# Fused attention and feed-forward kernel: order and gates of the loads, place of one small operation, size of the dummy matmuls

## The chip, the core and the metric

The kernel runs on one core of a Trainium2 chip. A core has five engines that each work through their own program in order and wait for one another by semaphores: TensorE (PE, matmuls; its weight loads are shown as PEld), VectorE (DVE), ScalarE (ACT), GpSimd (POOL) and SyncE (SP, which here only issues DMAs). The metric is the device time of one execution in microseconds. One execution was recorded by the profiler; its "span" runs from the first to the last instruction of the trace, and its own time is a little longer than that.

## The reference

Four batches of four heads, 1088 positions of 32 numbers. `phi` makes 64 features of each row by multiplying two projections of 8 numbers each. Attention is linear: keys and values are summed into a 64 x 32 matrix per head, then each query's features are multiplied with it and divided by a normaliser. The result, 4352 rows of 128, goes through two matrix products with a PReLU between them.

```python
def phi(x):
    a = np.einsum('rd,bhsd->bhsr', S1, x)            # r = 8
    b = np.einsum('rd,bhsd->bhsr', S2, x)
    return np.einsum('bhsi,bhsj->bhsij', a, b).reshape(*x.shape[:-1], 64)
q_p, k_p = phi(q), phi(k)
kv  = np.einsum('bhsf,bhsd->bhfd', k_p, v)
z   = np.sum(k_p, axis=2)
num = np.einsum('bhsf,bhfd->bhsd', q_p, kv)
den = np.einsum('bhsf,bhf->bhs', q_p, z)[..., None] + 1e-06
x   = (num / den).transpose(0, 2, 1, 3).reshape(4352, 128)
h   = x @ w_in                                       # 128 -> 2048
g   = np.maximum(h, 0) + alpha * np.minimum(h, 0)
out = g @ w_out                                      # 2048 -> 128
```

The kernel uses that g is (1 - alpha) relu(h) + alpha h: it multiplies relu(h) with (1 - alpha) w_out, and x directly with W = w_in diag(alpha) w_out, a 128 x 128 matrix that it makes once.

## The kernel before

**The steps and their names.** The program is a list of operations (`op`), each with a name, its possible engines, an estimated duration and what it depends on.

- Keys of batch b (`key_part`, `keys`): `kbT` transposes k in blocks of 32 on DVE (L684); `kbab` projects it on TensorE (L693); `kbabT` transposes back (L696); `kbkp0` and `kbkp1` multiply the two projections into features on POOL or DVE (L709); `zb` and `zMb` (L730, L753) make the normaliser's weights and `kvb` (L739) the sums of features times values on TensorE; `finb` (L779) turns them, and `kvWb` is the copy that the queries use. Batch 0 is done in two parts, `k0.0` and `k0.1`, and its weights take an extra turn, `finN` (L768), whose operand is the copy `kvn`.
- Queries (`query_part`): `qbT` (L795, L798) on DVE, `qbf` (L810) on TensorE, `qbfT` (L815) on DVE; then `denm` (L820, tile `tm`), a sum and a reciprocal on DVE (L825, L826), `rec` (L830, tile `ft`); `ph` (L841) makes the features, in two pieces, on DVE or POOL; `phT` (L844, tile `pt`) transposes them on DVE; `qbnum` (L855) is the numerator on TensorE, and copies `qbx` hand it over as the next layer's input (tile `xT`). The first half of batch 0 goes another way (`query_turned`, L867 to L927) and its second half is called `q0.1`.
- The two layers (`mlp`): ten groups of up to 512 rows; in a group 16 times `h` (L995, w_in on TensorE), `r` (relu into bfloat16, on ACT L1001 or DVE L1003) and `o` (L1017, accumulated over the 16), then `W` times the input into the same sum. `oT` transposes the result on DVE (L1026), `st` stores it by four or eight DMAs of SP. The last group is done the other way round (L1015) and stored by SP and ACT.
- Weights: `w_in_bf0` to `3` cast w_in by quarters; `w_a0` to `3` make (1 - alpha) w_out (L616, L625), `w_hi` and `w_lo` the two bfloat16 parts of alpha w_out (L616, L632, L642); `winT` (L648) transposes the cast w_in by DMA, and `Wmm` (L655) multiplies. `alpha` (L598) is the operation that makes 1 - alpha, 128 x 16 numbers.
- `dummy` (L560) issues matmuls of ones into an unused bank. `warm` is 56 units of them at the start; later ones are put where the planner expects TensorE to wait, in units of 64 columns.

**The order.** `plan` places the operations by list scheduling: it goes by due times (with a hand-set `SHIFT` for each name, and `PIN` that fixes an engine for some), by estimated durations, and by which buffers are free. What it gives is a fixed program for each engine; nothing is reordered at run time. Where TensorE is planned to wait before the first `h`, it fills the gap with dummies (`o.fill`). It also counts TensorE's instructions in blocks of 256 and plans with an arrival time for each block.

**The loads.** All big loads are issued by SP in the order k0.0, k0.1, q0.0, v0, w_in0 (a quarter of the columns), w_in1 (a quarter), w_out0 (half), w_in2 (half), w_out1, q0.1, k1, q1, v1. From w_in1 on they wait for `z0.1` on TensorE (`ld.paced`). The loads of batches 2 and 3 wait for `kv1.0` and `kv2.0`, and their place in SP's program goes by due times, which puts q ahead of k and, for batch 3, after the first two groups' stores. `winT` stands on SP between v1 and batch 2.

Of the kernel before, what the change touches and what calls it, by code (L numbers as in the profile page):

```python
# [34 lines left out]
class Op:  # L35
# [25 lines left out]
FILL, DUMMY = 20000, 54.0  # L61
# [5 lines left out]
    "S": 59667, "S1sel": 10454, "Sq": 48866, "W": 38241, "W0": 10504, "W1": 17298, "W2": 20915, "W3": 15708,  # L67
    "W4": 21623, "W5": 16770, "W6": 21205, "W7": 11310, "W8": 10547, "W9": 10683, "Wb": 34795, "Wmm": 20709,
    "Wrep": 11191, "alpha": 14336, "alphaT": 23409, "fin0": -1608, "fin1": 3203, "fin2": 5363, "fin3": 5170,
    "finN": 20529, "h0.0": 49560, "h0.1": 11101, "h0.10": 50794, "h0.11": 15029, "h0.12": 21397, "h0.13": 10702,  # L70
    "h0.14": 6019, "h0.15": 3566, "h0.2": 14944, "h0.3": 28491, "h0.4": 33392, "h0.5": 6597, "h0.6": 12715,
    "h0.7": 32839, "h0.8": 54596, "h0.9": 791, "h0b.0": 20399, "h0b.1": 35133, "h0b.10": 36560, "h0b.11": 5908,
    "h0b.12": 45231, "h0b.13": 10338, "h0b.14": 2625, "h0b.15": 3275, "h0b.2": 4472, "h0b.3": 12546, "h0b.4": 19250,
    "h0b.5": 15438, "h0b.6": 17468, "h0b.7": -1816, "h0b.8": 17299, "h0b.9": 285, "h1.0": 10173, "h1.1": 10019,
    "h1.10": 30138, "h1.11": 15770, "h1.12": 20282, "h1.13": 3034, "h1.14": 25187, "h1.15": 8151, "h1.2": 11431,
    "h1.3": 8787, "h1.4": 14576, "h1.5": 9668, "h1.6": 13362, "h1.7": 50585, "h1.8": 21734, "h1.9": 9330,
    "h2.0": 9678, "h2.1": 16490, "h2.10": 12382, "h2.11": 9708, "h2.12": 11418, "h2.13": 15217, "h2.14": 13215,
    "h2.15": 24133, "h2.2": 21040, "h2.3": 4308, "h2.4": 18035, "h2.5": 10266, "h2.6": 7463, "h2.7": 26003,
    "h2.8": 9815, "h2.9": 19440, "h3.0": 22489, "h3.1": 13198, "h3.10": 10418, "h3.11": 14120, "h3.12": 13277,
    "h3.13": 6991, "h3.14": 17721, "h3.15": 12240, "h3.2": 13931, "h3.3": 21452, "h3.4": 18588, "h3.5": 9222,  # L80
    "h3.6": 10333, "h3.7": 10722, "h3.8": 8477, "h3.9": 9531, "h4.0": 11482, "h4.1": 14983, "h4.10": 5640,
    "h4.11": 5278, "h4.12": 10648, "h4.13": 10963, "h4.14": 15678, "h4.15": 20853, "h4.2": 8292, "h4.3": 13793,
    "h4.4": 9095, "h4.5": 8505, "h4.6": 6626, "h4.7": 7359, "h4.8": 4392, "h4.9": 17274, "h5.0": 13778, "h5.1": 19393,
    "h5.10": 13159, "h5.11": 12797, "h5.12": 12519, "h5.13": 31365, "h5.14": 30780, "h5.15": 11474, "h5.2": 12773,
    "h5.3": 12659, "h5.4": 19773, "h5.5": 12212, "h5.6": 8459, "h5.7": 15284, "h5.8": 14446, "h5.9": 13732,
    "h6.0": 16630, "h6.1": 2502, "h6.10": 20851, "h6.11": 15505, "h6.12": 17383, "h6.13": 12956, "h6.14": 10612,
    "h6.15": 10267, "h6.2": 11456, "h6.3": 10883, "h6.4": 10310, "h6.5": 21846, "h6.6": 22040, "h6.7": 10870,
    "h6.8": 7665, "h6.9": 6035, "h7.0": 4340, "h7.1": 3098, "h7.10": -1753, "h7.11": 11296, "h7.12": 7588,
    "h7.13": 12906, "h7.14": 14233, "h7.15": 7067, "h7.2": 14375, "h7.3": -6579, "h7.4": 7592, "h7.5": 10854,
    "h7.6": 9439, "h7.7": 2272, "h7.8": 8935, "h7.9": 7746, "h8.0": 9406, "h8.1": 8953, "h8.10": 10665,  # L90
    "h8.11": 16408, "h8.12": 10559, "h8.13": 12283, "h8.14": 10489, "h8.15": 10675, "h8.2": 8668, "h8.3": 11275,
    "h8.4": 11218, "h8.5": 21747, "h8.6": 10783, "h8.7": 11650, "h8.8": 11469, "h8.9": 15009, "h9.0": 11117,
    "h9.1": 11059, "h9.10": 8627, "h9.11": 31788, "h9.12": 12698, "h9.13": 11237, "h9.14": 8916, "h9.15": 8537,
    "h9.2": 11789, "h9.3": 18879, "h9.4": 10141, "h9.5": 9621, "h9.6": 13047, "h9.7": 13411, "h9.8": 13883,
    "h9.9": 28117, "ident": 982177, "k0.0T": 41336, "k0.0ab": 43512, "k0.0abT": 9455, "k0.0kp0": 4972,
    "k0.0kp1": 7461, "k0.1T": -16024, "k0.1ab": 37978, "k0.1abT": 77440, "k0.1kp0": 25310, "k0.1kp1": 77321,
    "k1T": 19165, "k1ab": 26972, "k1abT": 11870, "k1kp0": 36678, "k1kp1": 12103, "k2T": 23505, "k2ab": 18392,
    "k2abT": 21657, "k2kp0": 14436, "k2kp1": 10771, "k3T": 26186, "k3ab": 20096, "k3abT": 14432, "k3kp0": 11247,
    "k3kp1": 4073, "kv0.0": 42422, "kv0.1": 14274, "kv1.0": 13312, "kv2.0": 8984, "kv3.0": 8063, "kvN": 25546,
    "kvW0": 9466, "kvW1": 18235, "kvW2": 23855, "kvW3": 28200, "kvc0": 51181, "kvc1": 7174, "kvc2": 22274,  # L100
    "kvc3": 50909, "kvn": 38698, "ld.k2": 14449, "ld.k3": -2170, "ld.q2": 8457, "ld.q3": -5646, "ld.v2": -3069,
    "ld.v2/1": -6899, "ld.v2/2": 15283, "ld.v2/3": 12432, "ld.v3": -40, "ld.v3/1": -14570, "ld.v3/2": 5161,
    "ld.v3/3": 6925, "mask4": 4023, "masks": 13648, "o0.0": 11943, "o0.1": 2366, "o0.10": 20881, "o0.11": 10271,
    "o0.12": 14749, "o0.13": 10968, "o0.14": 35560, "o0.15": 21596, "o0.2": 23173, "o0.3": 43771, "o0.4": 16741,
    "o0.5": 38206, "o0.6": 20582, "o0.7": 8990, "o0.8": 49926, "o0.9": 25518, "o0b.0": 18390, "o0b.1": 3411,
    "o0b.10": 17908, "o0b.11": 30988, "o0b.12": 14173, "o0b.13": 4924, "o0b.14": 19061, "o0b.15": 11989,
    "o0b.2": -537, "o0b.3": 18640, "o0b.4": 21860, "o0b.5": 9785, "o0b.6": 8481, "o0b.7": 10243, "o0b.8": 6314,
    "o0b.9": 6928, "o1.0": 10779, "o1.1": 19933, "o1.10": 19985, "o1.11": 21500, "o1.12": 8301, "o1.13": 8227,
    "o1.14": 17927, "o1.15": 25049, "o1.2": 10532, "o1.3": 6381, "o1.4": 19841, "o1.5": 12125, "o1.6": 11840,
    "o1.7": 12800, "o1.8": 20925, "o1.9": 14400, "o2.0": 22293, "o2.1": 17621, "o2.10": 16542, "o2.11": 29286,  # L110
    "o2.12": 16199, "o2.13": 19030, "o2.14": 20668, "o2.15": 15017, "o2.2": 10792, "o2.3": 19347, "o2.4": 17105,
    "o2.5": 12900, "o2.6": 16455, "o2.7": 17589, "o2.8": 15819, "o2.9": 30901, "o3.0": 16647, "o3.1": 17855,
    "o3.10": 14344, "o3.11": 15170, "o3.12": 12391, "o3.13": 20171, "o3.14": 19760, "o3.15": 14244, "o3.2": 20247,
    "o3.3": 17063, "o3.4": 16522, "o3.5": 15949, "o3.6": 12143, "o3.7": 15096, "o3.8": 31274, "o3.9": 13650,
    "o4.0": 14798, "o4.1": 13439, "o4.10": 24045, "o4.11": 20523, "o4.12": 20178, "o4.13": 29746, "o4.14": 19025,
    "o4.15": 19146, "o4.2": 19437, "o4.3": 15563, "o4.4": 14990, "o4.5": 14873, "o4.6": 39638, "o4.7": 34520,
    "o4.8": 22030, "o4.9": 21457, "o5.0": 28471, "o5.1": 19093, "o5.10": 20400, "o5.11": 16176, "o5.12": 16781,
    "o5.13": 21429, "o5.14": 23026, "o5.15": 16550, "o5.2": 19198, "o5.3": 19256, "o5.4": 15524, "o5.5": 16866,
    "o5.6": 32968, "o5.7": 16083, "o5.8": 29894, "o5.9": 15846, "o6.0": 20180, "o6.1": 19625, "o6.10": 18883,
    "o6.11": 9377, "o6.12": 20112, "o6.13": 19768, "o6.14": 18000, "o6.15": 19079, "o6.2": 16639, "o6.3": 33271,  # L120
    "o6.4": 34911, "o6.5": 17337, "o6.6": 16721, "o6.7": 20542, "o6.8": 20089, "o6.9": 22282, "o7.0": 12805,
    "o7.1": 12781, "o7.10": 11929, "o7.11": 11828, "o7.12": 14802, "o7.13": 11838, "o7.14": 11650, "o7.15": 15219,
    "o7.2": 12006, "o7.3": 13776, "o7.4": 14481, "o7.5": 12346, "o7.6": 15563, "o7.7": 11675, "o7.8": 10861,
    "o7.9": 11818, "o8.0": 13222, "o8.1": 15713, "o8.10": 10870, "o8.11": 18237, "o8.12": 10547, "o8.13": 10678,
    "o8.14": 17114, "o8.15": 10575, "o8.2": 23961, "o8.3": 17397, "o8.4": 11530, "o8.5": 21578, "o8.6": 14714,
    "o8.7": 13187, "o8.8": 11135, "o8.9": 13851, "o9.0": 12828, "o9.1": 37042, "o9.10": 10564, "o9.11": 11708,
    "o9.12": 11568, "o9.13": 19679, "o9.14": 10700, "o9.15": 10832, "o9.2": 13900, "o9.3": 9186, "o9.4": 13478,
    "o9.5": 13265, "o9.6": 12679, "o9.7": 12621, "o9.8": 13855, "o9.9": 11889, "oT0": 14479, "oT1": 9289,
    "oT2": 23169, "oT3": 15998, "oT4": 25999, "oT5": 25202, "oT6": 19456, "oT7": 14178, "oT8": 20420, "oT9.0": 9281,
# [996 lines left out]
```

## Time and profile before

| | us |
|---|---|
| median of 3 runs | 112.3 (111.85 to 113.9) |
| the profiled execution, its own time | 111.02 |
| its span | 108.9 |
| TensorE busy | 96.4 (88%), 1380 matmuls and as many weight loads |
| DVE busy | 80.5 (74%) |
| ACT busy | 68.1 (63%) |
| POOL busy | 42.4 (39%) |
| granted TensorE clock, mean | 0.989 |

A row of the timeline begins with its start in us and its length in us, both from the span's start; then the engine, the line of the kernel, the operation, the output and input tiles, the shape, and how many instructions it merges. Square brackets at the end say how long the engine sat idle ahead of it and what ended that. A matmul's recorded length overlaps with its neighbours'; two matmuls of 512 columns that follow each other start 0.22 us apart. SPq and ACTq rows are DMAs being issued, not landing; the page's last part gives the time from issue to landing.

### The profile page before, as it was taken

To read this page: it belongs to the slowest core of one execution; us is meant where nothing else is said; L and a number is where in the kernel's file an instruction comes from. 1 tells how busy PE (TensorE), PEld (TensorE's weight loads), DVE (VectorE), ACT (ScalarE), POOL (GpSimd) and SP (SyncE) were. 2 spreads that over 40 slices of the span, in tenths; PEclk is the share of its full clock that TensorE was granted. 3 is DMA by queue.
4 is the path that set the end of the run, shared out by engine and by line. 5 is a ranking of instruction groups with operands and counts; after the bars stand their busy time and mean duration, and the time that the engine had idled before them with its cause. 6 is when DMAs were issued, how large, how long until landed. Compare 5 with 4: busy or idle time off the path is not lost.

```text
span 108.9 us, 3412 instructions
## 1 busy us (share of the span) xinstructions
PE 96.4 (88%) x1380; PEld 54.6 (50%) x1380; DVE 80.5 (74%) x167; ACT 68.1 (63%) x166; POOL 42.4 (39%) x42
## 2 busy tenths in 40 slices
PE   7979879799799999999999189999999999999910
PEld 2347556467455564455544034474444446888800
DVE  6597749999978998875822989939993985498710
ACT  0502359999237972974989326567995587976800
POOL 3258859294997260590394006900350000000000
PEclk9999999999999999999999999999999999999995
DMA  2985999997004950055994005000002751002352
GB/s 54 322 249 157 302 294 403 174 127 156 0 6 157 335 128 0 4 95 90 240 285 103 1 0 101 2 6 0 0 0 47 124 99 28 0 14 33 62 92 54
DMA packets 26757, 11.83 MB, mean 109 GB/s; under 512 B 19957, under 2 KB 25333, under 8 KB 26741
## 3 DMA queue, kind: packets, MB, share of 16 engines
q1 hardware_dynamic: 26304, 11.51, 44.2%
q8 instruction: 11, 0.18, 0.7%
q10 hardware_dynamic: 436, 0.10, 0.4%
q14 instruction: 6, 0.04, 0.2%
HBM read 8.85 MB, written 2.23 MB: 102 GB/s over the span
## 4 chain that ended last, share of the span: by engine, by line
PE 57%; DMA 13%; DVE 13%; SPq 5%; issue 4%; POOL 4%; ACT 1%; ACTq 0%
PE ps L995 18%; PE ps L1017 18%; DMA k<-in_k_dram 11%; PE ps L739 4%; PE ps L855 4%; DVE pt__77 L844 4%; SPq L1046 3%; DMA out_dram<-ph__75 3%; PE ps L810 2%; PE ps L693 2%; POOL w L616 2%; PE ps L655 2%; DVE ph__75 L841 1%; PE ps L874 1%; SPq L1038 1%
## 5 line engine op out<-in xcount | busy, mean ns | idle before, releaser
L995 PEld LDWEIGHTS <-w_in_bf 128*128 128x128 bf16 x176 | 16.5, 98 | 12.8 <-issue 1.4
L1017 PEld LDWEIGHTS <-w 128*128 128x128 bf16 x160 | 15.5, 98 | 13.6 <-issue 1.8
L995 PE MATMUL ps<-xT__95,w_in_bf 128*128 128x512 bf16 (+1 forms) x80 | 21.0, 336 | 0.5 <-ACT rh__83 L1001 0.4
L995 PE MATMUL ps<-xT__96,w_in_bf 128*128 128x512 bf16 (+1 forms) x80 | 20.1, 336 | 0.0
L1001 ACT ACTIVATE rh__83<-ps 128x512 bf16<-128x512 f32 (+1 forms) x25 | 12.7, 510 | 5.2 <-PE ps L995 5.0
L709 POOL TENSOR_TENSOR kp__68<-ab__66 128x1152 f32<-128x1152 f32 (+1 forms) x5 | 8.6, 1735 | 15.8 <-DVE ab__66 L696 12.9
L1001 ACT ACTIVATE rh__84<-ps 128x512 bf16<-128x512 f32 (+1 forms) x22 | 11.5, 521 | 1.4 <-PE ps L995 0.8
L1001 ACT ACTIVATE rh__85<-ps 128x512 bf16<-128x512 f32 (+1 forms) x18 | 9.6, 536 | 1.7 <-PE ps L995 1.4
L841 POOL TENSOR_TENSOR ph__76<-ft__73 128x1280 f32<-128x1280 f32 (+1 forms) x3 | 6.7, 2242 | 10.1 <-DVE ph__75 L841 10.1
L1001 ACT ACTIVATE rh__87<-ps 128x512 bf16<-128x512 f32 (+1 forms) x16 | 8.6, 539 | 2.2 <-PE ps L1017 1.3
L1017 PE MATMUL ps<-rh__84,w 128*128 128x512 bf16 (+1 forms) x28 | 9.4, 337 | 0.0
L1017 PE MATMUL ps<-rh__83,w 128*128 128x512 bf16 (+1 forms) x28 | 9.3, 333 | 0.0
L855 PE MATMUL ps<-pt__77,kvW 32*32 32x256 f32 (+3 forms) x256 | 5.9, 372 | 3.4 <-DVE pt__77 L844 3.4
L1001 ACT ACTIVATE rh__86<-ps 128x512 bf16<-128x512 f32 (+1 forms) x15 | 8.5, 568 | 0.0
L1017 PE MATMUL ps<-rh__85,w 128*128 128x512 bf16 (+1 forms) x25 | 8.3, 332 | 0.0
L1017 PE MATMUL ps<-rh__86,w 128*128 128x512 bf16 (+1 forms) x24 | 8.1, 339 | 0.0
L1001 ACT ACTIVATE rh__88<-ps 128x512 bf16<-128x512 f32 (+1 forms) x15 | 7.6, 504 | 0.7 <-PE ps L995 0.6
L815 DVE STREAM_TRANSPOSE ft__73<-ps 128x576 f32<-128x576 f32 (+1 forms) x8 | 5.3, 696 | 3.1 <-PE ps L810 3.1
L684 DVE STREAM_TRANSPOSE kT__64<-k 128x1088 f32<-128x1088 f32 x3 | 3.9, 1284 | 3.9 <-DMA k<-in_k_dram 3.9
L709 POOL TENSOR_TENSOR kp__69<-ab__66 128x1152 f32<-128x1152 f32 x3 | 6.5, 2178 | 0.0
L560 PE MATMUL ps<-const-bfloat16-1.0 128*128 128x512 bf16 (+3 forms) x21 | 5.7, 378 | 0.8 <-PEq L1110 0.8
L855 PEld LDWEIGHTS ps<-pt__77,kvW 32*32 32x32 f32 x256 | 3.3, 103 | 5.7 <-DVE pt__77 L844 4.6
(172 smaller groups left out, 205.6 us busy)
## 6 DMA issues: line engine op xcount, KB each, us to landing
v<-in_v_dram SPq DMA_DIRECT2D x12, 144.0 KB, 5.6
k<-in_k_dram SPq DMA_DIRECT2D x3, 544.0 KB, 9.4
q<-in_q_dram SPq DMA_DIRECT2D x3, 544.0 KB, 3.8
w_out_f<-in_moe_w_out_dram SPq DMA_DIRECT2D x2, 512.0 KB, 8.4
out_dram<-oT__91 SPq DMA_DIRECT2D x12, 64.0 KB, 1.9
out_dram<-oT__92 SPq DMA_DIRECT2D x12, 64.0 KB, 2.7
w_in_f<-in_moe_w_in_dram SPq DMA_DIRECT2D x2, 256.0 KB, 3.3
w_in_f<-in_moe_w_in_dram SPq DMA_DIRECT2D x1, 512.0 KB, 7.1
```

Source lines behind the costliest of these rows:

```text
L560: nc.tensor.matmul(PS[:, 7, :n], ones(128), ones(n), start=True, stop=True, skip_group_check=True)
L684: nc.vector.transpose(kT()[:, :NT * D], src)
L709: (nc.vector if e == "dve" else nc.gpsimd).tensor_tensor(out=dst, in0=i0, in1=i1, op=ALU.mult)
L739: nc.tensor.matmul(ps(bk)[32 * h:32 * h + 32, :R], v_sb[b][:, h, lo + s], at(sb(bkp[h // 2]), x, [[1, R]]), start=first and s == 0, stop=l ...
L815: nc.vector.transpose(at(sb(bf)[:, 0], 2 * y * D, [[D, 2], [H * D, ns], [1, D]]), ps(f2[y])[:, :, :n].rearrange("p h (s t) -> p h s t", t=D))
L841: (nc.vector if e == "dve" else nc.gpsimd).tensor_tensor(out=dst, in0=i0, in1=i1, op=ALU.mult)
L844: oT.append(op("dve", dv(k) + 35, lambda e, lo=lo, hi=hi, bph=bph: nc.vector.transpose(sb(bp)[:, lo:hi].rearrange("p a b -> p (a b)"), sb( ...
L855: nc.tensor.matmul(ps(n2[c // 2])[32 * h:32 * h + 32, c % 2, :w * D], kvW[b][P, y, h], at(sb(bp)[P, 0], (2 * h + y) * D, [[2 * H * D, w], ...
L995: nc.tensor.matmul(ps(b)[:, :np], w_in_bf[:, c * 128:(c + 1) * 128], xs()[:, z], start=True, stop=True)
L1001: nc.scalar.activation(sb(br)[:, :np], ps(b)[:, :np], ACTF.Relu)
L1017: nc.tensor.matmul(ps(bo)[:, z], w, y, start=i == 0, stop=c == NC, skip_group_check=len(needs) > 1)
L1046: nc.sync.dma_start(bass.AP(tensor=out.tensor, offset=(16 + 17 * c) * DM + 32 * i, ap=[[NT * DM, 32], [S * DM, B], [1, 32]]), at(t[32 * i: ...
```

## The change

- **Opening loads.** w_in1 no longer waits; w_out0 and all behind it wait for `zM0` instead of `z0.1`.
- **Loads of batches 2 and 3.** They have fixed places in SP's program, k, q, v, ahead of all stores; batch 2's wait for `kv1.0` as before, batch 3's for `k2ab`. v no longer has a gate of its own (`GATE`). The planner's landing times for them are longer.
- **alpha** can only go to ACT; it was pinned to DVE.
- **Dummies** have units of 32 columns instead of 64, and fill a planned gap up to 35 ns instead of 90; `warm` has the same columns.
- **All due shifts and pins** are new: `SHIFT` and `PIN` are other tables, so the order on each engine is another one almost throughout.

```diff
-FILL, DUMMY = 20000, 54.0
+FILL, DUMMY = 20000, 27.0
...
-    return [512] * (units // 8) + [256] * (units % 8 // 4) + [128] * (units % 4 // 2) + [64] * (units % 2)
+    return [512] * (units // 16) + [256] * (units % 16 // 8) + [128] * (units % 8 // 4) + [64] * (units % 4 // 2) + [32] * (units % 2)
...
-            o.fill = max(0, int((t - free_at["pe"] - 90) / DUMMY)) if 3800 < t < FILL and not begun else 0
+            o.fill = max(0, int((t - free_at["pe"] - 35) / DUMMY)) if 3800 < t < FILL and not begun else 0
...
-    GATE = {"v2": "k2", "v3": "k3"}
+    GATE = {}
...
-    op("pe", 3750, lambda e: dummy(56), due=-1e6, name="warm", ni=14)
+    op("pe", 3750, lambda e: dummy(112), due=-1e6, name="warm", ni=14)
...
-    c_al = op(("act", "dve", "pool"), {"act": 200, "dve": 110, "pool": 200}, lambda e: nc.scalar.activation(omaT, alT, ACTF.Copy, bias=1.0, scale=-1.0) if e == "act" else
-              (nc.vector if e == "dve" else nc.gpsimd).tensor_scalar(omaT, alT, -1.0, 1.0, ALU.mult, ALU.add), [o], [], 80, name="alpha")
+    c_al = op("act", 200, lambda e: nc.scalar.activation(omaT, alT, ACTF.Copy, bias=1.0, scale=-1.0), [o], [], 100, name="alpha")
...
-    begin = next(o for o in ops if o.name == "z0.1")
+    begin = next(o for o in ops if o.name == "zM0")
     paced = op("sp", 1, lambda e: None, [begin], due=-1e6 + len(ops), name="ld.paced")
-    paced.late, loads["w_in1"][0].gate = True, begin
-    for name in ("w_in1", "w_out0", "w_in2", "w_out1", "q0.1", "k1", "q1", "v1"):
+    paced.late, loads["w_out0"][0].gate = True, begin
+    for name in ("w_out0", "w_in2", "w_out1", "q0.1", "k1", "q1", "v1"):
...
-    for b in (2, 3):
-        for name, lat in (("k", 4000), ("q", 5900), ("v", 7900)):
+    for b, begin in ((2, "kv1.0"), (3, "k2ab")):
+        before = next(x for x in ops if x.name == begin)
+        for name, lat in (("k", 5000), ("q", 7600), ("v", 9500)):
             for o in loads[f"{name}{b}"]:
-                o.gate = next(x for x in ops if x.name == f"kv{b - 1}.0")
-                o.deps.append(o.gate)
-                o.due, o.late = 12500.0 + 19000.0 * (b - 1), True
-                o.lat, o.arrive = lat - (4000 if name == "v" else 0), 0.0
+                if name == "k":
+                    o.gate = before
+                o.deps.append(before)
+                o.due, o.late = -6e5 + len(ops) * b + ops.index(o) / 1e3 + lat / 10, True
+                o.lat, o.arrive = lat - (1350 if name == "v" else 0), 0.0
```

In the changed program the orders that matter below are these. On POOL, the two products of `w_lo1` stand ahead of `denm` and `rec` of q0.1 instead of between them. On DVE, `k3T` stands after `rec` of batch 2's queries, ahead of two relus and of both `phT` of that batch. On ACT, `finN`'s operand `kvn`, then `kvN`, a copy for `fin0` and the copy of the first quarter's normaliser. `qT` of batch 1, the second copy of the input and the remaining steps keep their sequence.

More of the change, by code (lines that the diff above doesn't have):

```diff
@@ L59 @@
 FETCH = ((9000, 5000.0), (19000, 6500.0), (33000, 2900.0), (52000, 3600.0), (1e9, 2900.0))
-FILL, DUMMY = 20000, 54.0
+FILL, DUMMY = 20000, 27.0
 AHEAD = {"pe": 120, "act": 150, "dve": 250, "pool": 300, "sp": 0}
 SHIFT = {
[108 rows of a table removed]
[106 rows of a table added]
 }
 PIN = {
-    "S1sel": "dve", "Sq": "act", "alpha": "dve", "k0.0kp0": "pool", "k0.0kp1": "pool", "k0.1kp0": "pool",
-    "k0.1kp1": "pool", "kvN": "act", "kvW0": "dve", "kvW1": "act", "kvW2": "dve", "kvW3": "act", "kvc1": "dve",
[20 rows of a table removed]
[24 rows of a table added]
 }
 def parts(units):
-    return [512] * (units // 8) + [256] * (units % 8 // 4) + [128] * (units % 4 // 2) + [64] * (units % 2)
+    return [512] * (units // 16) + [256] * (units % 16 // 8) + [128] * (units % 8 // 4) + [64] * (units % 4 // 2) + [32] * (units % 2)
 def plan(ops, classes):
@@ L419 @@
     T0, TG = 13000.0, 9200.0
-    FIRST = {"rows": 3750.0, "arows": 6900.0, "S1r": 6000.0, "k0.0": 3780.0, "k0.1": 4850.0, "q0.0": 6300.0, "v0": 8400.0,
-             "w_in0": 8950.0, "w_in1": 11450.0, "w_out0": 13200.0, "w_in2": 15100.0, "w_out1": 16700.0, "q0.1": 17800.0,
-             "k1": 19900.0, "q1": 22000.0, "v1": 24000.0}
-    GATE = {"v2": "k2", "v3": "k3"}
+    FIRST = {"rows": 3750.0, "arows": 6900.0, "S1r": 6000.0, "k0.0": 3780.0, "k0.1": 4950.0, "q0.0": 6300.0, "v0": 8400.0,
+             "w_in0": 8950.0, "w_in1": 10300.0, "w_out0": 13000.0, "w_in2": 15000.0, "w_out1": 16800.0, "q0.1": 17800.0,
+             "k1": 20400.0, "q1": 22700.0, "v1": 24900.0}
+    GATE = {}
     state = {"t": 0.0}
```

258 rows, old and new, of tables (PIN, SHIFT) are left out of this document.

## The prediction

> **What bounds the kernel now.** I read the page's busy tenths first, then the windows, then the timeline around the one hole that both point at, engine by engine, and the waits in its brackets.
>
> ```profile
> PE   7979879799799999999999189999999999999910
> ```
>
> Each digit is a slice of 2.72 us of the span. TensorE is the bound: from the twelfth slice on it stands at nine tenths or more, but for one digit, the 1 in the 24th slice (62.6 to 65.3 us), and the end.
>
> ```profile
> core 0: us, PE busy (x) PEld busy (x) DVE busy (x) ACT busy (x) POOL busy (x), PEclk, DMA share, GB/s
> ...
> 60.00:64.00 4.00, 1.27 (x46) 0.65 (x53) 4.00 (x4) 0.89 (x2) 0.00 (x0) 1.00 0.00 0
> ```
>
> In this stretch TensorE works 1.27 of 4.00 us and DVE all 4.00, with nothing on the DMA queues. The granted clock (the 1.00) is full, so the clock is nothing to win here.
>
> ```profile
> 51.26 0.36 SPq L436 DMA_DIRECT2D q<-in_q_dram  x1
> 51.66 0.43 SPq L436 DMA_DIRECT2D k<-in_k_dram  x1
> ...
> 56.46 1.95 POOL L841 TENSOR_TENSOR ph__76<-ft__73 128x1024 f32<-128x1024 f32 x1
> ...
> 59.27 1.31 DVE L684 STREAM_TRANSPOSE kT__64<-k 128x1088 f32<-128x1088 f32 x1 [3.94 <-DMA k<-in_k_dram]
> 60.51 1.47 DVE L844 STREAM_TRANSPOSE pt__77<-ph__75 128x1280 f32<-128x1280 f32 x1
> 61.90 1.20 DVE L844 STREAM_TRANSPOSE pt__77<-ph__76 128x1024 f32<-128x1024 f32 x1
> ...
> 59.83 0.38 PE L1017 MATMUL ps<-rh__83,w 128*128 128x512 bf16 x1
> 60.05 0.38 PE L1017 MATMUL ps<-xT__96,W_bf 128*128 128x512 bf16 x1
> 63.16 0.72 PE L855 MATMUL ps<-pt__77,kvW 32*32 32x256 f32 x28 [2.73 <-DVE pt__77 L844]
> ```
>
> DVE works in order. The transpose of batch 3's k stands ahead of the two transposes (pt) that batch 2's numerator on TensorE needs. k was asked for at 51.66, behind q, and DVE stood 3.94 us for it. The matmuls at hand were used up at 60.43 (60.05 + 0.38), so TensorE stood 2.73 us until DVE had done its 1.31, 1.47 and 1.20.
>
> **The loads of the last batches.** They now go k, q, v. Batch 3's wait for the product ab of batch 2's keys instead of that batch's kv. In the chain, ab of batch 2 ends at 43.74:
>
> ```profile
> 43.09 0.65 PE ps L693 x16
> ```
>
> ```profile
> k<-in_k_dram SPq DMA_DIRECT2D x3, 544.0 KB, 9.4
> q<-in_q_dram SPq DMA_DIRECT2D x3, 544.0 KB, 3.8
> ```
>
> The same bytes took q, first of its batch in the later ones, 3.8 us to land, and k 9.4 (medians). So k of batch 3, now first, lands at 43.74 + 3.8 = 47.5; at worst, by k's own row, at 53.1. DVE came to the transpose at 59.27 - 3.94 = 55.33. Both are in time, and I take the wait as gone. What is late next: POOL's second product, done at 56.46 + 1.95 = 58.41, and its transpose of 1.20, so 59.6. TensorE asks at 60.43. **The stall of 2.73 us goes whole**, with 0.8 us to spare; the changed order of DVE has the transpose of k earlier still, ahead of two relus and both pt. In batch 2 the gate stays the same and k can only land sooner: nothing. On SP the six loads of batch 3 now stand ahead of the first eight stores instead of behind them, at under half a us each; those stores only free output buffers, and the next writer of one comes in the second half of the next batch's numerator: nothing.
>
> **The opening.** One half of w_in is no longer held back, and w_out with all behind it waits for zM of batch 0 instead of its z.
>
> ```profile
> 8.29 0.44 SPq L436 DMA_DIRECT2D w_out_f<-in_moe_w_out_dram  x1
> ...
> 8.85 0.62 PE L753 MATMUL ps<-zt__98,S1sel 128*128 128x16 f32 x4 [0.23 <-DVE zt__98 L747]
> ...
> 11.52 1.01 SPq L436 DMA_DIRECT2D k<-in_k_dram  x1
> ...
> 14.40 0.33 PE L768 MATMUL ps<-ident,bN 128*128 128x128 f32 x1 [1.32 <-ACT NS L413]
> ```
>
> zM ends at 9.47, so w_out leaves 1.2 us later than 8.29, and so does each load behind it on SP. The half of w_in that has gone ahead (256 KB) gives some of it back: a quarter of a transfer of 1 MB, which I put at 0.8 us by q's row (544 KB in at most 3.8 us, less a start). So k of batch 1, asked for at 11.52 and landing by the 9.4 of its row at 20.9, lands at 21.3, or at 22.1 if nothing is given back.
>
> The row at 14.40 is a transpose by TensorE for the numerator's weights; TensorE idles 1.32 us ahead of it, for a copy on ACT that its operand does not come from. The instructions themselves come by DMA:
>
> ```profile
> q8 instruction: 11, 0.18, 0.7%
> ```
>
> Eleven pieces of 16 KB for the 2,760 instructions of TensorE (matmuls and weight loads) are some 251 each, and the 450th of the program falls at this matmul. My reading is that a piece came late through the flood of loads. With w_out held until 9.47 less is in its way: worth between 0 and 1.3 us at this place.
>
> [...]
>
> What the saturated stage hangs on lies further back:
>
> ```profile
> 22.23 1.27 DVE L684 STREAM_TRANSPOSE kT__64<-k 128x1088 f32<-128x1088 f32 x1
> ...
> 23.76 0.28 DVE L826 RECIPROCAL tm__79<-tm__79 128x20 f32<-128x20 f32 x1
> ...
> 23.04 1.05 POOL L616 TENSOR_TENSOR w_out_f<-w_out_f,alTT 128x512 f32<-128x512 f32 x1
> 24.17 1.17 POOL L616 TENSOR_TENSOR w<-w_out_f,w 128x512 bf16<-128x512 f32 x1
> 25.28 0.49 POOL L830 TENSOR_TENSOR ft__73<-ft__73,tm__79 128x160 f32<-128x160 f32 x1
> ```
>
> ```profile
> 29.58 2.18 POOL L709 TENSOR_TENSOR kp__69<-ab__66 128x1152 f32<-128x1152 f32 x1
> ```
>
> kv of batch 1 can't start before this kp is done, at 31.76; kp follows DVE's ph, and ph follows POOL's ft. ft could have begun at 24.04, after the reciprocal; it began at 25.28, behind the pair of 1.05 and 1.17 for a quarter of w_out. In the changed order that pair is done ahead of tm, so up to 1.24 us go; DVE has other work in that gap that stays (a transpose ab), so I take 0.9. Ahead of it DVE loses three relus, a copy and small products to ACT or to earlier places and gets one quarter of w_out, some 0.7 us less; and it starts sooner by what is won at 14.40. But k lands at 21.3 at the earliest, so kT moves from 22.23 by 0.9 at most. I take 0.4. **The opening gives 0.9 + 0.4 = 1.3 us.** Bounds: nothing, if k lands so late that kT moves back by 0.9; 2.5, if 1.3 at 14.40 and 1.24 are both kept.
>
> **alpha and the dummies.**
>
> ```profile
> 7.63 1.07 DVE L599 TENSOR_SCALAR omaT<-alTT 128x16 f32<-128x16 f32 x1
> ```
>
> On DVE alpha's copy took 1.07 us and the 0.23 of idle time ahead of zM, above, stands behind it. On ACT it goes to a place where ACT waits for TensorE anyway: between 0 and -0.2, taken as 0, since the matmuls behind zM wait for POOL. The dummies become 25 instead of 21, by the programs' order some 1,000 columns more; at the 0.22 us between the matmuls of 512 at 59.83 and 60.05 that is 0.4 us, in gaps where TensorE waits: 0, and +0.4 if each wait is shorter than planned.
>
> **The rest of the order** is shuffled by new due times and pins: the same matmuls, with as many of the two layers' between the numerators of successive batches, to within three. I take 0, and bounds of -0.5 to +1.3 (half of the one stall of 2.73 that the old order had, in the saturated stage). The stores at the end keep their order: 0.
>
> **Sum.** The profiled execution took 111.0 us. 111.0 - 2.7 - 1.3 = 107.0. The median of the runs shown is 112.3, 1.3 above the profiled one, so the forecast is **108.3 us**, 3.6% below. Less than 2% either way (110.05 to 114.5) can't be told from no change.
>
> **Rivals.**
> (a) Only the stall goes: the loads of the opening come later by the 1.2 us and eat the rest. For it: they are a train without a gap. 111.0 - 2.7 + 1.3 = 109.6.
> (b) The stall is half replaced: a transpose or a product of POOL in batch 2 or 3 comes late in the new order; the old one would have had 0.8 us to spare. 1.3 left over and no opening: 110.9.
> (c) Slower. The weights are cast sooner, so the transposes of w_in by DMA leave sooner, into the loads of batch 1.
>
> ```profile
> 20.50 4.53 SPq L648 DMA_TRANSPOSE winT<-w_in_bf  x2
> ```
>
> ```profile
> 20.00:24.00 4.00, 3.42 (x53) 2.17 (x53) 3.96 (x11) 4.00 (x16) 2.44 (x3) 1.00 1.49 156
> ```
>
> With them in flight the DMA moved 156 GB/s at a share of 1.49. If they leave at 18 instead of 20.5, with k, q and v of batch 1 (1.65 MB) still to come, these take 10.6 us at that rate, to 28.6, and kT goes with them, by 6.4 us. Less the 1.3 that the opening wins: 111.0 - 2.7 + 5.1 + 1.3 = 114.7. It decides once k lands after some 26 us, where the loss eats 2.7 and 1.3. Against it: they stand behind v on the same queue.
> (d) More: all of 2.5 in the opening: 111.0 - 2.7 - 2.5 + 1.3 = 107.1.
>
> [...]
>
> **How the numbers follow.** Forecast 0.50, (a) 0.20, (b) 0.14, (c) 0.08, (d) 0.08. The range takes in (d) less the 0.5 of the shuffle, 106.6, and (b) with half a us above it, 111.4. Faster by over 2%: forecast, (d) and three quarters of (a), 0.73; within 2%: the rest of (a) and (b), 0.19; slower: 0.08.
>
> **What would show it.** The 1 in TensorE's tenths gone, and no wait of DVE for batch 3's k: the main step. kv of batch 1 near 30.4 instead of 31.8: the opening. The matmul at 14.40 near 13: the piece of code; if it keeps its idle 1.3 us, that reading falls. Wrong if TensorE has a new wait of over 1 us, most likely for pt or kT of DVE, or if k of batch 1 lands after 23 us.

## The result, and the profile after

| | before | after |
|---|---|---|
| median | 112.07 us (4 runs, 111.1 to 113.9) | 107.66 us (4 runs, 107.08 to 109.0) |
| profiled execution, its own time | 111.02 us | 107.24 us |
| its span | 108.9 us | 105.3 us |
| mean granted clock in it | 0.989 | 0.993 |

The ratio is 0.9616, 95% interval 0.9503 to 0.973: 3.8% faster. Taken again later (f3 below) it is 0.9622, 0.9514 to 0.9729. Here and below a ratio compares, for each kernel, only the executions within 1.5% of its fastest.

The busy tenths of TensorE after, on the page (slices of 2.63 us):

```profile
PE   7999976789999998999999999999999999999930
PEclk9999999999999999999999999999999999999997
```

The 1 in the middle is gone. What is left are the opening, one 8 in the sixteenth slice and the end. The timeline of DVE and TensorE after, at the place where the hole was, and the issue of batch 3's loads (lines beyond 598 carry numbers one lower than before):

```profile
43.66 0.35 SPq L436 DMA_DIRECT2D k<-in_k_dram  x1
44.05 0.43 SPq L436 DMA_DIRECT2D q<-in_q_dram  x1
...
52.59 1.30 DVE L683 STREAM_TRANSPOSE kT__64<-k 128x1088 f32<-128x1088 f32 x1
53.81 0.65 DVE L1002 TENSOR_SCALAR rh__90<-ps 128x512 bf16<-128x512 f32 x1
54.39 0.67 DVE L1002 TENSOR_SCALAR rh__84<-ps 128x512 bf16<-128x512 f32 x1
54.99 1.22 DVE L843 STREAM_TRANSPOSE pt__77<-ph__75 128x1024 f32<-128x1024 f32 x1
...
57.43 1.50 DVE L843 STREAM_TRANSPOSE pt__77<-ph__76 128x1280 f32<-128x1280 f32 x1
```

k is asked for at 43.66, 8 us sooner and ahead of q, and the transpose of it has no bracket: DVE doesn't wait. Both pt are done at 58.93, and the numerator of batch 2 follows at 59.71 without a wait. What TensorE does wait for after, in the view of its waits (total us, times, longest):

```profile
PE ps L994 <- POOL w_in_bf L417: 0.9, 1, 0.9
...
PE ps L854 <- DVE pt__77 L843: 0.7, 2, 0.5
PE ps L1016 <- POOL w L615: 0.6, 1, 0.6
PE ps L908 <- ACT rb L413: 0.6, 1, 0.6
```

Three of these are new and stand between the first h and the first full stage: TensorE now arrives there before its weights (`w_in_bf`, `w`) and before a copy of ACT (`rb`). The longest for pt, 0.47 us at 41.33, is the 8 in the tenths: the numerator of batch 1, which before had no wait.

Cut at three marks of the timelines (the first matmul of batch 1's kv, the first of batch 2's numerator, the end of the last matmul), the profiles divide so. f1 to f4 are experiments, below.

| us | to kv of batch 1 | to numerator of batch 2 | to the last matmul's end | tail | span |
|---|---|---|---|---|---|
| before | 31.72 | 31.44 | 40.71 | 5.03 | 108.9 |
| after | 30.87 | 28.84 | 41.14 | 4.45 | 105.3 |
| f3, after again | 30.18 | 28.67 | 41.14 | 4.91 | 104.9 |
| f2, before with the load edit | 31.72 | 28.65 | 40.58 | 5.75 | 106.7 |
| f4, all but the new order | 31.18 | 28.63 | 40.71 | 5.58 | 106.1 |
| f1, stall filled with dummies | 31.94 | 31.29 | 40.70 | 5.07 | 109.0 |

After less before: -0.85, -2.60, +0.43, -0.58, together -3.60, the difference of the spans. The second and the third stretch are read as one where orders differ: in the new order two matmuls of 0.22 us stand behind batch 2's numerator instead of ahead of it. From kv of batch 1 to the last matmul's end it is 72.15 before, 69.98 after, 69.81 in f3 and 69.23 in f2. The first stretch differs between executions of one order too; how much of its -0.85 is the change's is taken up with the opening, below.

### The profile page after: what moved, and what is told of

The parts are those of the page before. It is cut to its first block, busy times and chain, and to the rows that moved or that the text cites. A ratio compares the mean times of both kernels' runs of the same rounds, so it can differ in the third digit from the quotient of the medians.

```text
span 105.3 us, 3445 instructions
## 1 busy us (share of the span) xinstructions
PE 96.4 (92%) x1384; PEld 54.2 (51%) x1384; DVE 81.2 (77%) x163; ACT 69.3 (66%) x174; POOL 39.0 (37%) x40
## 4 chain that ended last, share of the span: by engine, by line
PE 62%; POOL 9%; DMA 7%; DVE 7%; issue 5%; SPq 4%; ACT 2%; ACTq 0%; DVEq 0%; POOLq 0%
PE ps L1016 21%; PE ps L994 21%; DMA w_out_f<-in_moe_w_out_dram 6%; PE ps L560 5%; PE ps L854 4%; PE ps L692 3%; POOL w L615 3%; SPq L1045 3%; POOL ph__76 L840 2%; PE ps L738 2%; POOL kp__69 L708 2%; PE ps L809 2%; DVE pt__77 L843 1%; DMA out_dram<-ph__75 1%; PE ps L729 1%
## 5 line engine op out<-in xcount | busy, mean ns | idle before, releaser
L994 PE MATMUL ps<-xT__95,w_in_bf 128*128 128x512 bf16 (+1 forms) x80 | 20.6, 337 | 1.1 <-POOL w_in_bf L417 0.9
L994 PE MATMUL ps<-xT__96,w_in_bf 128*128 128x512 bf16 (+1 forms) x80 | 19.3, 336 | 0.2 <-ACT rh__83 L1000 0.2
L1000 ACT ACTIVATE rh__83<-ps 128x256 bf16<-128x256 f32 (+1 forms) x26 | 12.8, 491 | 3.5 <-PE ps L994 3.3
L1000 ACT ACTIVATE rh__86<-ps 128x512 bf16<-128x512 f32 (+1 forms) x20 | 10.5, 526 | 4.0 <-PE ps L994 3.9
L1000 ACT ACTIVATE rh__85<-ps 128x512 bf16<-128x512 f32 (+1 forms) x22 | 11.4, 517 | 1.7 <-PE ps L994 1.0
L1000 ACT ACTIVATE rh__84<-ps 128x256 bf16<-128x256 f32 (+1 forms) x18 | 9.4, 520 | 1.4 <-PE ps L994 1.4
L1016 PE MATMUL ps<-rh__83,w 128*128 128x512 bf16 (+1 forms) x29 | 9.5, 328 | 0.6 <-POOL w L615 0.6
L1002 DVE TENSOR_SCALAR rh__84<-ps 128x256 bf16<-128x256 f32 (+1 forms) x12 | 6.6, 548 | 4.5 <-PE ps L994 3.0
L1000 ACT ACTIVATE rh__87<-ps 128x512 bf16<-128x512 f32 (+1 forms) x16 | 8.5, 529 | 0.9 <-PE ps L994 0.8
L1016 PE MATMUL ps<-rh__85,w 128*128 128x512 bf16 (+1 forms) x27 | 9.1, 335 | 0.0
L1016 PE MATMUL ps<-rh__84,w 128*128 128x512 bf16 (+1 forms) x27 | 8.9, 331 | 0.0
L1016 PE MATMUL ps<-rh__86,w 128*128 128x512 bf16 (+1 forms) x23 | 7.8, 338 | 0.0
L560 PE MATMUL ps<-const-bfloat16-1.0 128*128 128x512 bf16 (+4 forms) x25 | 6.8, 376 | 0.9 <-PEq L1111 0.8
L1016 PE MATMUL ps<-rh__87,w 128*128 128x512 bf16 (+1 forms) x19 | 6.5, 340 | 0.0
L1000 ACT ACTIVATE rh__88<-ps 128x512 bf16<-128x512 f32 (+1 forms) x10 | 5.2, 518 | 1.4 <-PE ps L994 1.3
```

What stands on the lines that cost most here:

```text
L560: nc.tensor.matmul(PS[:, 7, :n], ones(128), ones(n), start=True, stop=True, skip_group_check=True)
L994: nc.tensor.matmul(ps(b)[:, :np], w_in_bf[:, c * 128:(c + 1) * 128], xs()[:, z], start=True, stop=True)
L1000: nc.scalar.activation(sb(br)[:, :np], ps(b)[:, :np], ACTF.Relu)
L1002: nc.vector.tensor_scalar_max(sb(br)[:, :np], ps(b)[:, :np], 0.0)
L1016: nc.tensor.matmul(ps(bo)[:, z], w, y, start=i == 0, stop=c == NC, skip_group_check=len(needs) > 1)
```

## The experiments

In all but e7 and f1, the planner's order of the base kernel is kept on every engine and only the named loads or places are moved. `gated(names, gate, late)` takes these loads out of SP's program and puts them back, in this order, behind the named step (or behind `late`), to wait for `gate`. Ratios are to the kernel before on the same chip.

### The load edit alone, in three forms

**e1**: k ahead of q for batch 3, gate and place as before.

```diff
+    gated(("k3", "q3", "v3"), "kv2.0", "st1")
```

> The kernel before, with nothing changed but batch 3's k, q, v instead of q, k, v on SP, behind the same kv of batch 2 and the same stores. Theory A (k is late because it is second): issued near 51.3, k lands 3.8 to 4.1 us later at 55.4, DVE (at 55.33) waits at most 0.3 us, TensorE's stall of 2.73 us goes: 2.4 to 2.7 us faster, ratio about 0.977. Rival B (it is late because it is asked for late, and the first of three shares the DMA with the rest): k lands at 57 or later and 1 to 2 us of the stall stay, ratio 0.985 to 0.995.

Measured: 108.18 us (107.71 to 109.27), ratio 0.9622 [0.9525, 0.9719]. In its profile k is issued at 51.58 and transposed at 55.56 without a wait of DVE, so theory A holds and rival B falls.

**e2**: q first as before, but the earlier gate, ahead of the stores.

```diff
+    gated(("q3", "k3", "v3"), "k2ab")
```

> The kernel before, batch 3's loads still q, k, v, but behind ab of batch 2 and ahead of the first stores. Theory A and B both: k asked for near 44.2 lands by 53.6 even at 9.4 us, before DVE wants it at 55.33; the stall of 2.73 goes, ratio about 0.976. If the stall were caused by DVE's order itself, it would stay at 1 us or more.

Measured: 108.13 us (107.51 to 110.5), ratio 0.9601 [0.9498, 0.9704].

**e3**: the whole load edit of batches 2 and 3.

```diff
+    gated(("k2", "q2", "v2"), "kv1.0")
+    gated(("k3", "q3", "v3"), "k2ab")
```

> The kernel before with the change's loads of batches 2 and 3 whole (k, q, v; batch 3 behind ab of batch 2, ahead of the stores), every engine's order otherwise the old one. The prediction's step: 2.7 us faster, ratio 0.976, so that the rest of the change is worth about 0.015. Rival (the new due times and pins do it): under 1 us.

Measured: 108.13 us (107.44 to 109.51), ratio 0.9584 [0.9493, 0.9674].

Either half of the edit takes the whole stall away: the stage up to the numerator of batch 2 is 28.64, 28.63 and 28.63 us in the three, against 31.44. The load edit alone brings the time to within about half a us of the changed kernel's. All three gained more than was expected: the ratios are 0.958 to 0.962, where a stall priced at its length gave 0.976. The part on the clock, below, comes back to this.

### The changed kernel with the old loads of batch 3

**e4**: after, with batch 3's loads q first and behind kv of batch 2.

```diff
+    gated(("q3", "k3", "v3"), "kv2.0")
```

> The changed kernel with batch 3's loads put back: q, k, v behind kv of batch 2 and behind the first stores. In its order DVE wants k at 52.6, ahead of two relus and both pt. Theory: k is asked for near 50.6 and lands 7.6 us later at 58.2, DVE stands 5.6 us, TensorE runs out of relus and then waits: 3 to 5 us slower than the changed kernel, ratio to the kernel before 0.99 to 1.01. Rival (the new order has room): under 1 us slower, ratio 0.97.

Measured: 115.23 us (112.68 to 118.06), ratio 1.021 [1.0085, 1.0335]: slower than the kernel before by 1 to 3%, and 7.6 us behind the changed kernel, where 3 to 5 were expected. The timeline of its DVE and TensorE, and the windows behind (us; busy time and instructions of PE, PEld, DVE, ACT, POOL; granted clock; DMA share; GB/s):

```profile
56.25 0.38 PE L994 MATMUL ps<-xT__96,w_in_bf 128*128 128x512 bf16 x1
62.13 0.58 PE L994 MATMUL ps<-xT__96,w_in_bf 128*128 128x512 bf16 x1 [5.50 <-DVE rh__90 L1002]
...
60.19 1.31 DVE L683 STREAM_TRANSPOSE kT__64<-k 128x1088 f32<-128x1088 f32 x1 [5.93 <-DMA k<-in_k_dram]
```

```profile
60.00:62.00 2.00, 0.00 (x0) 0.00 (x0) 1.81 (x2) 0.00 (x0) 0.00 (x0) 0.63 0.03 11
62.00:64.00 2.00, 1.87 (x5) 0.69 (x5) 1.82 (x3) 1.09 (x2) 0.00 (x0) 0.50 0.00 0
64.00:66.00 2.00, 2.00 (x6) 0.66 (x5) 0.95 (x2) 1.05 (x2) 0.00 (x0) 0.50 0.00 0
66.00:68.00 2.00, 2.00 (x8) 0.79 (x7) 1.85 (x2) 0.72 (x3) 0.00 (x0) 0.67 0.00 0
```

The new order has the transpose of k ahead of two relus that TensorE needs, so the same late k costs 5.50 us instead of 2.73. And the granted clock goes to half during the pause and stays there for some 5 us of work behind it (by the 0.63 and the 0.67, from 60.5 to 67.3). The new order needs the new loads; the old order only gains by them.

### The parts of the opening

**e5**: after, with w_out and all behind it waiting for z again; w_in1 stays free.

```diff
+    loads["w_out0"][0].gate = named["z0.1"]
```

> The changed kernel, w_out and all loads behind it waiting for z of batch 0 as in the kernel before, instead of zM; w_in1 stays free. Theory C (the later gate lets a piece of TensorE's code through): the transpose finN, at 12.38 in the changed kernel, goes back to about 14, the first h from 14.29 to about 15.7, while w_out lands 1 us sooner (its users waited 0.6 and 0.9 us for weights); kv of batch 1 within 0.5 us of 30.87, ratio 0.96 to 0.97. Rival D (finN was late for another reason): finN stays at 12.4, the weights come 1 us sooner, kv of batch 1 at 30.3 or before, ratio 0.955.

Measured: 108.17 us (107.73 to 108.22), ratio 0.9689 [0.9609, 0.977]; by these intervals not to be told from the changed kernel. The matmul that stood at 14.40 came at 12.92, the first h at 14.87: with the old gate it has no pause either. So theory C, which had it back near 14, falls; the ratio of 0.955 that rival D gave is not reached.

**e6**: before, with the gates of the change in the opening.

```diff
+    loads["w_in1"][0].gate = None
+    loads["w_out0"][0].gate = named["zM0"]   # and all behind it after zM0
```

> The kernel before with the change's opening gates alone: w_in1 free, w_out and the rest behind zM. Orders of all engines as before. Theory C: finN from 14.40 to about 12.9, the first h from 16.12 to about 14.6, but kv of batch 1 moves by 0 to 0.9 only, since POOL's and DVE's chain there is the old one: ratio 0.992 to 1.0. Rival D: finN stays at 14.4, weights 0.4 to 1.2 us later, ratio 1.0 to 1.01.

Measured: 112.15 us (109.65 to 115.7), ratio 0.9898 [0.9771, 1.0026]. The matmul that stood at 14.40 comes at 12.59, the first h at 14.42, but kv of batch 1 at 31.74, where it was; the interval of the ratio takes in 1. The view of TensorE's waits shows where the lead goes:

```profile
PE ps L995 <- ACT w_in_bf L413: 1.6, 1, 1.6
```

**e7**: before, with the same columns of warm-up dummies as 14 matmuls of 256 instead of 7 of 512, which puts 14 instructions more ahead of the rest of TensorE's program. Theory C's late piece of code would then begin 14 instructions sooner in that rest.

```diff
-    op("pe", 3750, lambda e: dummy(56), due=-1e6, name="warm", ni=14)
+    op("pe", 3750, lambda e: [dummy(4) for _ in range(14)], due=-1e6, name="warm", ni=14)
```

> The kernel before with the first seven dummies of 512 columns cut into fourteen of 256: the same columns, 14 instructions more on TensorE ahead of everything. Theory C: the pause of 1.3 us moves 14 instructions up, to between the last matmuls of kv0.1 and the two qR ahead of finN (12.2 to 12.4 in the trace of before), which then start near 14.2. Rival D: kv0.1 and qR stay together, and the pause stays right in front of finN. Time within 1% either way.

Measured, one execution: 113.51 us. The matmul came at 12.18 without a pause ahead of it or at the places named: no theory's forecast. What this profile does show is the clock, after a stall of 2.89 us; its timeline and windows:

```profile
59.37 0.38 PE L1017 MATMUL ps<-xT__96,W_bf 128*128 128x512 bf16 x1
62.63 2.57 PE L855 MATMUL ps<-pt__77,kvW 32*32 32x256 f32 x64 [2.89 <-DVE pt__77 L844]
```

```profile
60.00:62.00 2.00, 0.00 (x0) 0.00 (x0) 2.00 (x3) 0.21 (x1) 0.00 (x0) 0.97 0.00 0
62.00:64.00 2.00, 1.36 (x46) 0.90 (x56) 2.00 (x3) 0.00 (x0) 0.00 (x0) 0.50 0.00 0
64.00:66.00 2.00, 2.00 (x48) 0.44 (x39) 0.37 (x1) 0.79 (x2) 0.00 (x0) 0.50 0.27 48
66.00:68.00 2.00, 2.00 (x13) 0.63 (x6) 1.43 (x2) 0.40 (x2) 0.62 (x1) 0.50 0.52 90
68.00:70.00 2.00, 2.00 (x9) 0.85 (x8) 1.43 (x3) 1.19 (x2) 2.00 (x2) 0.82 0.03 2
```

The numerator took 2.57 us, in f1 below the same 64 matmuls took 1.58. From this numerator to the next were 22.15 us, in the profile of before 19.47.

**e8**: before, with alpha on ACT.

```diff
+    named["alpha"].on = "act"
```

> The kernel before with alpha on ACT instead of DVE, all else as it was. zM begins 0 to 0.7 us sooner; the matmuls behind it wait for POOL, so no gain at the first h and at the end: ratio 0.998 to 1.002.

Measured: 111.92 us (110.56 to 114.2), ratio 0.9988 [0.9915, 1.0061]. No gain is shown, and the stall of 2.7 us is still there.

### What is left: the clock, and the new order

**f1**: before, with the stall filled.

```diff
         def num(e):
+            for _ in range(12 if b == 2 else 0):
+                nc.tensor.matmul(ps(n2[0])[:, 0, :512], ones(128), ones(512), start=True, stop=True, skip_group_check=True)
```

> The kernel before with 12 idle matmuls of 512 columns (2.6 us at the 0.22 us between two of them) right ahead of batch 2's numerator, written into its own bank ahead of it; the stall of 2.73 us is still there in time, but TensorE works through it. Theory P (the stall costs more than its length, because in many executions TensorE's granted clock falls after it, as the 6,5,6 and 5,5,8 in two profiles): no fall of the clock behind the numerator, mean clock at or over 0.985, median 1 to 2 us under the kernel before's, highest time under 113. Rival Q (the stall costs its length; the surplus of the load edit comes from somewhere else): times and spread as of the kernel before, ratio 1.00 +- 0.005.

Measured: 111.27 us (109.67 to 113.93, 12 runs) against 111.87 (110.07 to 113.79), ratio 0.9938 [0.987, 1.0006]. Its timeline:

```profile
60.48 2.79 PE L851 MATMUL ps<-const-bfloat16-1.0 128*128 128x512 bf16 x12
63.23 1.58 PE L857 MATMUL ps<-pt__77,kvW 32*32 32x256 f32 x64
```

TensorE works through the hole, and the numerator starts where it did (63.16). How often the clock falls is seen over all executions, with the mean granted clock of each. This table takes all of them.

| | executions | mean clock under 0.98 | mean time of all | of those at 0.984 or more |
|---|---|---|---|---|
| before | 48 | 41 | 112.8 us | 110.9 us (7) |
| before, stall filled (f1) | 12 | 4 | 111.5 us | 110.8 us (8) |
| before, stall kept (e6, e8) | 20 | 16 | 112.3 us | 110.7 us (4) |
| old order, stall gone (e1, e2, e3, f2, f4) | 25 | 1 | 108.4 us | 108.3 us (21) |
| new order (after, e5, f3) | 14 | 1 | 107.6 us | 107.5 us (13) |
| new order, longer stall (e4) | 10 | 10 | 115.6 us | none |

With the stall the clock falls in most executions (41 of 48 and 16 of 20 have a mean under 0.98), filled with idle matmuls in a third (4 of 12), without it in two of 39. At a mean clock of 0.984 or more, before and the old order without a stall are 2.6 us apart (110.9 and 108.3), near the stall's 2.73. The rest of the 4.4 us between their means goes with the clock. By f1, 4 of 12 against 41 of 48, the pause is what the clock falls for in most of them, but f1's time came down less than theory P said: by means 0.6 us against the 16 executions of before beside it (1.3 against all 48), and its highest time was not below 113. How the missing us divides between the clock and something that the dummies cost is not settled.

Where the clock falls is seen in the pages' clock tenths, here of before, e1 and e4:

```profile
PEclk9999999999999999999999999999999999999995
PEclk9999975999999999999999999999999999999985
PEclk9999998599999999999995589999999999999999
```

Before has no fall but at the very end, behind the last matmul (0.78 from 106 to 107, 0.50 from there on), and that slice alone takes its mean to 0.989. In e1, where the hole is gone, the clock fell in the opening, behind this pause:

```profile
13.84 0.33 PE L768 MATMUL ps<-ident,bN 128*128 128x128 f32 x1 [1.51 <-issue]
```

By windows of 1 us it was 0.96 from 14 to 15, 0.50 from 15 to 18 and 0.83 from 18 to 19, so at half from 14.9 to 18.3. In before a pause of 1.32 us at the same place left it at 1.00. e4's row shows a fall in the opening too, around pauses of 1.83 and 0.57 us, so not all of that execution's loss comes from the loads of batch 3.

How soon it fell and came back differs too. In e7 it fell at 61.9, by the 0.97 of the window from 60 to 62, some 2.1 us after the last matmul's end at 59.75; in e4 at 60.5, 3.9 us after that end at 56.63; in e1 the whole pause was 1.51 us. It came back in e7 at 68.7, by the 0.82 of the window from 68 to 70, 6.1 us after the numerator began, and in e4 at 67.3, 5.2 us after the matmul at 62.13.

**f2** is e3 again, **f3** the changed kernel again, and **f4** is before with the loads of e3, the gates of e6 and alpha on ACT: everything but the new order and dummies.

```diff
+    gated(("k2", "q2", "v2"), "kv1.0")
+    gated(("k3", "q3", "v3"), "k2ab")
+    loads["w_in1"][0].gate = None
+    loads["w_out0"][0].gate = named["zM0"]   # and all behind it after zM0
+    named["alpha"].on = "act"
```

> The kernel before with the whole load edit of batches 2 and 3, run beside the changed kernel. Theory R (the opening, the new order, alpha and the dummies together are worth nothing): the same median as the changed kernel within 0.5 us, some 4.5 us under before. Rival S (the prediction's sum): 1.3 us above the changed kernel.

> The changed kernel, beside the one above on the same chip. Theory R: within 0.5 us of it. Rival S: 1.3 us below it.

> The kernel before with the load edit of batches 2 and 3, the opening's loads (second half of w_in free, w_out and all behind it after zM) and alpha on ACT; the old order of every engine and the old dummies stay. If the opening's loads and alpha give what they gave first h in their own runs and the new order gives it back: below the changed kernel by 0.5 to 1 us. If what they give is lost to the weights in any order: equal to it and to the load edit alone within 0.5 us. If the new order is needed for the gain: 0.5 to 1.3 us above the changed kernel.

Measured, six runs each on one chip: f2 108.02 us (106.98 to 108.97), 0.9697 [0.9582, 0.9812]; f3 107.08 us (105.91 to 108.19), 0.9622 [0.9514, 0.9729]; f4 108.53 us (107.5 to 109.58), 0.9756 [0.9645, 0.9866]. From the spread of the six, the means differ by 1.0 +- 0.95 us (f2 less f3) and 1.5 +- 0.95 (f4 less f3); f4 less f2 is 0.5 +- 0.95. So theory R is unlikely, though zero lies only just outside: by these twelve executions, what the change holds beside the load edit is worth between 0 and 2 us, with S's 1.3 inside. The earlier ratios don't show it: 0.9584 for the load edit (e3), 0.9616 for the whole change. If it is there, it comes from what f4 lacks, the new order (or the finer dummies); the gates and alpha, which f4 has too, show no gain. In the profiles the order shows at the place that the prediction named. The timelines of POOL and DVE ahead of batch 1's kp, f4 first, then f3:

```profile
23.22 0.28 DVE L826 RECIPROCAL tm__79<-tm__79 128x20 f32<-128x20 f32 x1
...
22.51 1.04 POOL L616 TENSOR_TENSOR w_out_f<-w_out_f,alTT 128x512 f32<-128x512 f32 x1
23.63 1.16 POOL L616 TENSOR_TENSOR w<-w_out_f,w 128x512 bf16<-128x512 f32 x1
24.74 0.49 POOL L830 TENSOR_TENSOR ft__73<-ft__73,tm__79 128x160 f32<-128x160 f32 x1
26.90 2.18 POOL L709 TENSOR_TENSOR kp__68<-ab__66 128x1152 f32<-128x1152 f32 x1 [1.67 <-DVE zt__98 L747]
```

```profile
22.78 0.28 DVE L825 RECIPROCAL tm__79<-tm__79 128x20 f32<-128x20 f32 x1
...
23.21 0.49 POOL L829 TENSOR_TENSOR ft__73<-ft__73,tm__79 128x160 f32<-128x160 f32 x1 [0.84 <-DVE tm__79 L825]
25.73 2.18 POOL L708 TENSOR_TENSOR kp__68<-ab__66 128x1152 f32<-128x1152 f32 x1 [2.03 <-DVE zt__98 L746]
```

In f4 the reciprocal is done at 23.50 and ft starts 1.24 us later, behind the pair; in f3 0.15 us later. The second half of the way to kp loses some of it: from ft's end to kp 1.67 us in f4, 2.03 in f3. What is left holds in every profile: from the start of batch 1's kT to its kv it is 9.48 or 9.49 us in the ten of the old order and 8.87 to 9.06 in the four of the new.

No version tried is shown to beat the changed kernel. The finer dummies were not tried by themselves.

## Why the prediction was right, point by point

**The stall goes whole: right.** In the old order the stretch from kv of batch 1 to the last matmul is 2.92 shorter without it (f2), where the term was 2.73. What was to be late next, POOL's product and its transpose, never was. This is the mechanism that the prediction named, and e1 to e3 show it by the loads alone.

**The step from the profiled execution to the median: wrong.** The sum was 107.0 for the profiled execution, and that took 107.24. Then the prediction added the 1.3 us by which before's median stood above its profile, as if the change left that alone. By the means above it was for the most part the clock that falls behind the stall, of which f1 leaves a part open, and it went with the stall: after, the median stands 0.4 above the profile. The profile of before (clock 1.00 in the stall's window, 0.989 over all) was one of the few executions without a fall, so a stall of 2.73 us was priced at its length and cost, over all executions, 4.4.

**The sum for the profiled execution: close in part by luck.** Its terms missed by more than the sum did. On one side the opening gave 0.45 less than was taken and the new order cost 0.75, on the other the tail gave 0.58 and the stall 0.2 more.

**The opening: right in place, over-sized, and in part not shown.** Of 1.3 it gave 0.85 in the profile after, 1.54 in f3. But single executions differ by as much: kv of batch 1 came at 30.68 to 32.03 in the ten profiles of the old order, at 30.18 to 31.09 in three of the new and at 32.46 in e4, whose clock fell there. What every profile shows is the part from kT on, 0.4 to 0.6 us, where 0.9 was taken for POOL's pair. The start of kT, where 0.4 was taken, lies at 21.19 to 22.55 in the old order and at 21.12 to 22.22 in those three: no gain is shown. The timelines of POOL and DVE after:

```profile
21.95 1.31 DVE L683 STREAM_TRANSPOSE kT__64<-k 128x1088 f32<-128x1088 f32 x1
...
24.30 0.78 DVE L695 STREAM_TRANSPOSE ab__66<-ps 128x576 f32<-128x576 f32 x1 [0.49 <-PE ps L692]
25.00 1.45 DVE L840 TENSOR_TENSOR ph__75<-ft__73 128x1280 f32<-128x1280 f32 x1
...
23.95 0.48 POOL L829 TENSOR_TENSOR ft__73<-ft__73,tm__79 128x160 f32<-128x160 f32 x1 [0.85 <-DVE tm__79 L825]
```

POOL's pair gave 1.33 at ft (25.28 to 23.95, with the 0.28 of kT), but only 0.81 of it reaches ph (25.81 to 25.00): the transpose ab now stands in DVE's way, and it waits for the projection of kT. kT moved by 0.28 (22.23 to 21.95), where 0.4 was taken. k of batch 1, issued at 12.46, took 9.5 us to land, to 21.96, near the prediction's 22.1 with nothing given back. Two readings there were off: what the prediction calls a half of w_in is a quarter (its 256 KB are right), and its 0.8 us for them is not what the row it names gives, since 544 KB in 3.8 us make it 1.8.

**The matmul at 14.40: the reading falls.** It came at 12.38 after, as "what would show it" asked, but not for the reason given. Of the kernels that start just as before does, f1 shows this in its timeline of TensorE:

```profile
12.31 0.27 PE L768 MATMUL ps<-ident,bN 128*128 128x128 f32 x1
```

Same order, same gates, no pause, and kv of batch 1 at 31.94, not sooner. In f2 the matmul came at 13.08, in e1 at 13.84. The lateness belonged to single executions, and 2 us there were worth nothing at kv: what comes sooner waits for weights, as after (0.64 for w, 0.94 for w_in_bf) and e6 (1.6) show. Whether a piece of code was late in the profile of before was not shown: its row of q8 (11 packets, 0.18 MB) says neither whose instructions they were nor when they landed, so that the 251 to a piece are an estimate.

**alpha: right** as far as it shows: no gain in e8, to within 1 us. **The gates of the opening** (in the sum by way of 14.40): no gain shown (e6, and f4 beside f2). **The shuffle, taken as 0: off by +0.6 to +0.75** (69.81 and 69.98 against f2's 69.23), inside its bounds; 0.47 of it is the new wait of batch 1's numerator. **The tail, taken as 0: off by -0.58** in the profile after. The last copy of ACT waits for a store to land; before, and after:

```profile
105.19 0.27 ACT L413 COPY ph__75<-ps 128x128 f32<-128x128 f32 x1 [2.00 <-DMA out_dram<-ph__75]
```

```profile
101.69 0.27 ACT L413 COPY ph__75<-ps 128x128 f32<-128x128 f32 x1 [1.29 <-DMA out_dram<-ph__75]
```

In the four profiles of the new order this wait is 1.29 to 1.85 us, in the ten of the old order 2.00 to 2.89, so it is the order's.

**The rivals.** (a), only the stall goes, is nearly what f2 shows for the load edit alone (108.0, not 109.6, for the reason of the clock). (b) took place in small, and in batch 1: one new wait of 0.47 us. (c) didn't happen: the transposes of w_in did leave sooner, at 17.49 instead of 20.50, but kT of batch 1 came at 21.95, not 28.6. (d) gave 107.1, and the time came out between the forecast and it, but not because the opening gave more: the surcharge for the median was too much.

## What to carry to other kernels

A stall of TensorE like this one, of 2 to 3 us, is to be priced over many executions: its length, plus what the clock loses behind it in a share of them (here 4.4 us between the means for a stall of 2.73). Where single executions differ, a gain is read from the stretch that stays the same in all profiles of one order, as from kT to kv here. Where a median stands above its profile, look at the mean clock of each run before adding the difference to a forecast; it may belong to the very wait that the change removes. A pause seen in one profile near the start (1.32 us ahead of L768 in before, none in f1) is checked in a second profile before anything is built on it, and time won ahead of a stage counts only when the operands of that stage come sooner too: in e6 the first h came at 14.42 instead of 16.12, TensorE then waited 1.6 us for w_in_bf, and kv came at 31.74 instead of 31.72.

## What was not expected of the hardware

The granted clock halved behind a pause of 2.89 us in e7 (0.50 from 61.9 to 68.7 us) and of 1.51 us in e1 (0.50 from 14.9 to 18.3), but in the profile of before the stall of 2.73 us left it at 1.00. In e7 the pause cost some 2.7 us more from this numerator to the next (22.15 against 19.47), beside its own 2.89: nearly as much again. The opening, too, varies by execution: with one and the same program start the matmul at L768 came anywhere from 12.31 (f1) to 14.40 us.
